# Two matmul groups of a fused FFT and two-layer MoE kernel, issued one and one instead of one after the other

## Chip, cores and metric

One core of a Trainium2 chip runs the whole kernel. The metric is the device time of one execution in microseconds (us); the time before is the median of three runs. Every row below comes from one profiled execution of the kernel before.

## What is computed

The reference takes x of 8 x 3072 x 256 and does three things in turn:

```python
X = np.fft.fft(np.fft.fft(x, axis=1), axis=2).real   # 24576 rows of 256
h = X @ w_in                                         # first layer, 256 -> 2048
x2 = (h - np.tanh(h)) @ w_out                        # 2048 -> 256
h2 = x2 @ w_in2                                      # second layer, 256 -> 1024
solu = h2 * softmax(h2)                              # then a layer norm with gain g_ln
out = layernorm(solu) * g_ln @ w_out2                # 1024 -> 256
```

The weights of the two layers are given as double-precision words and are narrowed in the kernel.

## The kernel before

A first stage of some 195 us does the transform along the sequence and prepares the weights; it is not touched. Then a main loop of 768 steps does both layers (`for step in range(steps + 2)`, L943). The rows of X come in 48 groups of 512 (`n`), and a group takes 16 steps, one for each 128 of the 2048 columns of the first layer (`j` or `m`). A product of two numbers in single precision is made of three passes of the fast 32-bit type: high by high, high by low and low by high (`PASSES`). So every 128-deep product is three matmuls, and each matmul has its own load of weights.

In a step TensorE is given these groups of matmuls, in this order:

- `ab` (L720), 6 matmuls 256 columns wide: the first layer's first product, for this step;
- from `layer2` (L919), by the step's number modulo 4 (`q`): in q = 0 and 1 `h2` (L806), 6 matmuls 512 wide, the second layer's first product for a tile of 128 rows; in q = 2 and 3 `outp` (L896), 12 matmuls 256 wide, the second layer's second product (the output) of an earlier tile, one half of its depth in each of the two steps;
- `o1` (L773), 6 matmuls 512 wide: the first layer's second product, for the step two back. It adds all 16 steps of a group up in two PSUM banks (`x2p`).

The program order is written out by hand (the tile framework is told to keep it), and each engine works its own list in order. What the groups wait for: `o1` reads `gh`, of which ScalarE rounds the high part (L762, shown under its helper's line L152) and GpSimd (POOL) subtracts the low part (L762 through `rest`, L155). The passes of `o1` are high weight, low weight, and last the one with the low part of `gh`, two matmuls each. `outp` reads `ut`, made in the same way in q = 0 and 1 (`split_moved`, L867). At the end of a tile (q = 3) ScalarE scales the output (`o`, L905) and SyncE sends it off (L907). After the last step of a group `o1` copies `x2p` out (L789 to L793: two copies `x2f` and two roundings `x2s` on ScalarE, two subtractions on POOL); this falls in j = 1. In j = 9 and 11 POOL and ScalarE also prepare the input of the next group (`split_z`, L225).

The helper `weave` (L180) takes generators and runs one item of each in turn until all are done. A tail after the loop (L998 to L1024) does the last tiles.

Of the kernel before, what the change touches and what calls it, by code (L numbers as in the profile page):

```python
# [29 lines left out]
NG = B * GPB  # L30
NM = FF1 // P
# [96 lines left out]
def fft2_moe_moe_kernel(  # L128
# [22 lines left out]
    def rnd(o, i):  # L151
        nc.scalar.activation(out=o, in_=i, func=AF.Copy)  # L152

    def rest(eng, o, i, hi):
        eng.tensor_tensor(out=o, in0=i, in1=hi.bitcast(F32), op=ALU.subtract)  # L155
# [24 lines left out]
    def weave(*works):  # L180

        works = list(works)
        while works:
            works = [w for w in works if next(w, works) is not works]
# [366 lines left out]
    def split_wo1(c, raw):  # L551
        rnd(wo1[c][:, 0], raw)
        rest(nc.gpsimd, wo1[c][:, 1], raw, wo1[c][:, 0])
# [74 lines left out]
    def taken(banks, shape, tag, name):  # L628
        banks.append(banks.pop(0))
        return banks[-1].tile(shape, F32, tag=tag, name=name)  # L630
# [134 lines left out]
    def o1(n, m):  # L765
        if m == 0:
            x2p[n] = [p_x2.tile([P, 2 * GP], F32, tag=f"x2_{mt}", name=f"x2p{n}_{mt}") for mt in range(2)]
        gh = gs.pop((n, m))
        c, k = divmod(m, 4)

        for i, (hw, hg) in enumerate(((0, 0), (1, 0), (0, 1))):
            for mt in range(2):
                nc.tensor.matmul(  # L773
                    x2p[n][mt],
                    wo1[c][:, hw, k, mt * P : (mt + 1) * P],
                    gh[:, hg],
                    start=(m == 0 and i == 0),
                    stop=(m == NM - 1 and i == 2),
                )
        if m == NM - 1:  # L780
            xs = wk.tile([P, 2, 2, 2 * GP], F32R, tag="x2s", name=f"x2s{n}")
            x2s[n] = xs
            if n == NG - 1:
                for mt, p in enumerate(x2p.pop(n)):
                    rnd(xs[:, 0, mt], p)
                    rest(nc.vector, xs[:, 1, mt], p, xs[:, 0, mt])
                return
            xf = wk.tile([P, 2, 2 * GP], F32, tag="stage", name=f"x2f{n}")
            for mt, p in enumerate(x2p.pop(n)):  # L789
                rnd(xf[:, mt], p)  # L790
            for mt in range(2):
                rnd(xs[:, 0, mt], xf[:, mt])
                rest(nc.gpsimd, xs[:, 1, mt], xf[:, mt], xs[:, 0, mt])  # L793
# [28 lines left out]
    def soft(n, i):  # L822
        ph, e, st = h2s.pop((n, i)), es.pop((n, i)), sts[n, i]
        u = wk.tile([P, FF2], F32, tag="u", name=f"u{n}_{i}")
        nc.vector.scalar_tensor_tensor(  # L825
            out=u, in0=ph, scalar=1.0, in1=e, op0=ALU.mult, op1=ALU.mult, accum_out=st[:, 2:3]
        )
        nc.vector.tensor_scalar_mul(st[:, 3:4], st[:, 2:3], -1.0 / FF2)
        nc.vector.tensor_scalar_add(st[:, 4:5], st[:, 1:2], 1e-9)
        nc.vector.reciprocal(out=st[:, 5:6], in_=st[:, 4:5])  # L830
        us[n, i] = (u, e)

    def square(n, i):
        u, e = us[n, i]
        st = sts[n, i]
        nc.scalar.activation(out=e, in_=u, func=AF.Square, bias=st[:, 3:4], accum_out=st[:, 6:7])  # L836
        scale(n, i)
# [15 lines left out]
    def turn(n, i):  # L853
        u = us[n, i][0]
        t = mv.tile([P, FF2], F32, tag="t", name=f"tb{n}_{i}")
        nc.vector.transpose(out=t, in_=u)  # L856
        d = mv_d[(4 * n + i) % len(mv_d)]
        nc.sync.dma_start(out=d, in_=t)
        m = mv.tile([P, FF2], F32, tag="m", name=f"um{n}_{i}")
        blocks = d.rearrange("(q p) (k a j) -> a p k q j", q=4, a=4, j=32)  # L860
        for a in range(4):
            nc.sync.dma_start(
                out=m[32 * a : 32 * a + 32].rearrange("p (k q j) -> p k q j", q=4, j=32), in_=blocks[a]
            )
        moved[n, i] = m
# [21 lines left out]
    def outp(n, i, half):  # L887
        if half == 0:
            pos[n, i] = taken(bank_o, [P, 512], "t", f"po{n}_{i}")
        po = pos[n, i]  # L890
        ut = uts.pop((n, i, half))
        for k4 in range(4):
            k = half * 4 + k4
            ks = slice(k4 * P, (k4 + 1) * P)
            for q, (hu, hw) in enumerate(PASSES):
                nc.tensor.matmul(  # L896
                    po[:, :D],
                    ut[:, hu, ks],
                    wo2[:, hw, k],
                    start=(k == 0 and q == 0),  # L900
                    stop=(k == NK2 - 1 and q == 2),
                )
        if half == 1:
            o = wk.tile([P, D], F32, tag="o", name=f"o{n}_{i}")
            nc.scalar.activation(out=o, in_=po[:, :D], func=AF.Copy, scale=sts.pop((n, i))[:, 10:11])  # L905
            r0 = (n * 4 + i) * P
            nc.sync.dma_start(out=out[r0 : r0 + P, :], in_=o)  # L907
            us.pop((n, i))
            pos.pop((n, i))

    def tile_at(step, back):
        t = (step - NM - back) // 4
        return divmod(t, 4) if 0 <= t < 4 * NG else None
# [5 lines left out]
    def layer2(step):  # L919
        q = step % 4  # L920
        at = tile_at(step, 8)
        if at and q == 0:
            square(*at)
            if 4 * at[0] + at[1] <= last_moved:
                turn(*at)
        at = tile_at(step, 12)
        if at:
            if q < 2:
                split_moved(*at, q)
            else:  # L930
                outp(*at, q - 2)
        at = tile_at(step, 4)
        if at:
            if q < 2:
                h2(*at, q)
            elif q == 2:
                expo(*at)
            else:
                soft(*at)

    steps = NG * NM
    out_done = o1_done = 0
    for step in range(steps + 2):  # L943
        n, j = divmod(step, NM)
        if step < steps:
            pab = ab(n, j)
            asb = lead(n, j, pab) if n == 0 else None

        lag = 2 if step < NM else 1
        for s in range(out_done, min(step - lag + 1, steps)):  # L950
            act_out(*divmod(s, NM))
        out_done = max(out_done, min(step - lag + 1, steps))
        if step < steps:
            act_in(n, j, pab, asb or lead(n, j, pab))
        layer2(step)
        s1 = step - 4 if step < NM else step - 2
        for s in (range(o1_done, min(s1 + 1, steps))):
            o1(*divmod(s, NM))
        o1_done = max(o1_done, min(s1 + 1, steps))
        if step in (4, 8):  # L960
            c = (4, 8).index(step) + 2
            split_wo1(c, wo1_raw[c])
        if step == NM:
            raw1.close()
            mv = pool(ctx, "mv", 2, side="right")
        if step in (10, 12):
            split_wi2((step - 10) // 2)
        if step in (2, 3):
            load_wo2(step - 2)
        if step == 6:  # L970
            split_special()
        if 8 <= step < NM:
            gain_wo2(step - 8)
        if NM + 2 < step <= NM + 6:
            special_out(step - NM - 3, pa)
        if step == NM:
            cm = mean_wo2()
        if step == NM + 1:
            for half in range(2):
                center_wo2(half, cm)  # L980
        if NM + 2 <= step < NM + 6:
            pa = special(step - NM - 2)
        if NM + 2 <= step < NM + 4:
            split_wo2(step - NM - 2)
        if j == 6 and 1 <= n and n + 1 < NG:
            load_z(n + 1)
        if 1 <= n and n + 1 < NG and j in (9, 11):
            split_z(n + 1, int(j > 9))
# [9 lines left out]
    tiles = [(NG - 2, 3)] + [(NG - 1, i) for i in range(4)]  # L998
    expo(*tiles[0])
    for f in range(2):  # L1000
        outp(NG - 2, 1, f)
    evict = [trans(NG - 2, 2, f) for f in range(2)]
    for e in evict:
        e()
    for f in range(2):
        outp(NG - 2, 2, f)
    for f in range(2):
        h2(*tiles[1], f)
    soft(*tiles[0])
# [1 line left out]
    for i, at in enumerate(tiles):  # L1011
        evict = [trans(*at, f) for f in range(2)]
        square(*at)
        for e in evict:
            e()
        if i + 2 < len(tiles):
            for f in range(2):
                h2(*tiles[i + 2], f)
        if i + 1 < len(tiles):
            soft(*tiles[i + 1])  # L1020
        if i + 2 < len(tiles):
            expo(*tiles[i + 2])
        for f in range(2):
            outp(*at, f)  # L1024


def thrice(a):
# [45 lines left out]
```

## Time and profile before

| what | value |
|---|---|
| median of 3 runs | 2931.36 us (2930.78 to 2932.79) |
| the profiled execution's own time | 2932.95 us |
| its span in the trace | 2931.2 us |
| TensorE matmuls busy | 98% of the span |
| TensorE weight loads busy | 85% |
| VectorE, ScalarE, POOL busy | 82%, 62%, 67% |

In the rows PE is TensorE's matmuls and PEld its weight loads; DVE is VectorE and ACT ScalarE. A row of the timeline holds instructions of one kind that follow each other: start, length up to the end of the last, and how many. Matmuls are pipelined, so a group's length overlaps the next group's start; what a group takes of the path is the distance from its start to the next group's start.

### The profile page before, as it was taken

The page shows a single profiled execution, that of the slowest core. Times are in us where ns is not written, and L with a number is a line of the kernel's source. Part 1 is how long each engine was busy: PE and PEld are TensorE (multiplying, and loading weights), DVE is VectorE, ACT ScalarE, POOL GpSimd, SP SyncE. Part 2 cuts the span into 40 slices and gives each one's busy share as a digit, 9 for nine tenths or more (in the row PEclk, how much of TensorE's full clock was granted, in tenths as well). Part 3 has the DMA queues.
Part 4 walks back from the last instruction along what each step waited for, and adds up shares of the span by engine and source line. Part 5 has one row for each costly group of instructions (what it writes and reads, how often), then busy time and mean ns, then how long its engine had stood idle before and what let it go on. Part 6 is the DMA issues. An engine that isn't in the chain of part 4 may idle for free. (4 is left out here: it accounts for less than half of the span.)

```text
span 2931.2 us, 49792 instructions
## 1 busy us (share of the span) xinstructions
PE 2882.8 (98%) x16799; PEld 2482.5 (85%) x16799; DVE 2402.9 (82%) x4818; ACT 1804.3 (62%) x3287; POOL 1966.0 (67%) x2413
## 2 busy tenths in 40 slices
PE   7899999999999999999999999999999999999999
PEld 4467888888888888888888888888888888888888
DVE  7897888888888888888888888888888888888885
ACT  2345666666666666666666666666666666666665
POOL 0156767776677776777777767777677766777763
PEclk9999999999999999999999999999999999999999
DMA  8771333443334334344334433433433443443331
GB/s 309 261 285 31 89 92 94 93 94 89 94 87 99 87 89 99 89 93 93 88 94 91 95 89 93 95 90 89 94 93 90 92 92 89 94 97 90 89 91 42
DMA packets 876512, 303.75 MB, mean 104 GB/s; under 512 B 788520, under 2 KB 837688, under 8 KB 872960
## 3 DMA queue, kind: packets, MB, share of 16 engines
q1 hardware_dynamic: 873536, 293.95, 40.7%
q10 hardware_dynamic: 2304, 6.29, 0.5%
q8 instruction: 132, 2.16, 0.3%
q14 instruction: 124, 1.02, 0.1%
q0 software_dynamic: 416, 0.33, 0.0%
HBM read 162.01 MB, written 138.47 MB: 103 GB/s over the span
## 5 line engine op out<-in xcount | busy, mean ns | idle before, releaser
L155 POOL TENSOR_TENSOR gh<-g,gh 128x512 fp32r<-128x512 f32 x768 | 994.3, 1298 | 478.5 <-ACT gh L152 478.5
L773 PE MATMUL x2p<-gh,wo 128*128 128x512 f32 x4608 | 1203.9, 396 | 2.3 <-POOL gh L155 1.7
L773 PEld LDWEIGHTS x2p<-gh,wo 128*128 128x128 f32 x4608 | 838.3, 188 | 180.9 <-POOL gh L155 8.2
L749 ACT ACTIVATE t<-h 128x512 f32<-128x512 f32 x768 | 459.7, 599 | 558.0 <-DVE h L743 456.5
L720 PEld LDWEIGHTS ab<-zs,wt 128*128 128x128 f32 x4608 | 650.1, 188 | 72.8 <-DVE h L743 2.7
L720 PE MATMUL ab<-zs,wt 128*128 128x256 f32 x4608 | 669.1, 280 | 2.1 <-DVE h L743 2.1
L754 DVE TENSOR_TENSOR g<-h,t 128x512 f32<-128x512 f32 x768 | 521.6, 679 | 171.7 <-ACT t L749 168.1
L152 ACT ACTIVATE gh<-g 128x512 fp32r<-128x512 f32 x768 | 481.0, 626 | 235.7 <-DVE g L754 230.7
L806 PE MATMUL ph<-wi,x2s 128*128 128x512 f32 x2304 | 602.8, 397 | 9.7 <-DVE u L825 9.7
L896 PE MATMUL po<-wo,ut 128*128 128x256 f32 x4608 | 592.0, 278 | 3.5 <-ACT ut L152 2.8
L896 PEld LDWEIGHTS po<-wo,ut 128*128 128x128 f32 x4608 | 558.7, 188 | 5.3 <-ACT ut L152 3.5
L727 DVE SCALAR_TENSOR_TENSOR asb<-nb,wnu,ab 128x256 f32<-128x256 f32 x768 | 366.8, 478 | 230.7 <-PE ab L720 230.2
L155 POOL TENSOR_TENSOR ut<-um,ut 128x512 fp32r<-128x512 f32 x372 | 481.7, 1295 | 0.9 <-issue 0.9
L806 PEld LDWEIGHTS ph<-wi,x2s 128*128 128x128 f32 x2304 | 407.7, 189 | 83.6 <-PE ab L720 9.7
L743 DVE TENSOR_TENSOR h<-asb,ab 128x256 f32<-128x256 f32 x768 | 329.3, 429 | 26.5
L742 DVE TENSOR_TENSOR h<-asb,ab 128x256 f32<-128x256 f32 x768 | 329.2, 429 | 26.1
L819 ACT ACTIVATE e<-ph,st 128x1024 f32<-128x1024 f32 x192 | 214.3, 1116 | 98.2 <-DVE st L817 82.6
L817 DVE TENSOR_REDUCE st<-ph 128x1 f32<-128x1024 f32 x192 | 233.5, 1216 | 3.5 <-PE ph L806 3.5
L825 DVE SCALAR_TENSOR_TENSOR u<-ph,e 128x1024 f32<-128x1024 f32 x192 | 233.4, 1216 | 0.0
L152 ACT ACTIVATE ut<-um 128x512 fp32r<-128x512 f32 x372 | 231.0, 621 | 0.0
L856 DVE STREAM_TRANSPOSE tb<-u 128x1024 f32<-128x1024 f32 x186 | 230.1, 1237 | 0.0
L836 ACT ACTIVATE e<-u,st 128x1024 f32<-128x1024 f32 x192 | 219.5, 1143 | 0.0
(101 smaller groups left out, 1529.4 us busy)
## 6 DMA issues: line engine op xcount, KB each, us to landing
mv_d<-tb SPq DMA_DIRECT2D x186, 512.0 KB, 2.6
um<-mv_d SPq DMA_DIRECT2D x744, 128.0 KB, 3.8
out<-o SPq DMA_DIRECT2D x192, 128.0 KB, 1.7
x<-xr SPq DMA_DIRECT2D x23, 1024.0 KB, 8.0
z_d<-zt SPq DMA_DIRECT2D x16, 384.0 KB, 7.2
z_d<-zt ACTq DMA_DIRECT2D x16, 384.0 KB, 7.1
wo<-w_out SPq DMA_DIRECT2D x24, 256.0 KB, 5.3
zf<-z_d SPq DMA_DIRECT2D x48, 128.0 KB, 3.4
```

The lines of the kernel that those rows point to most:

```text
L152: nc.scalar.activation(out=o, in_=i, func=AF.Copy)
L155: eng.tensor_tensor(out=o, in0=i, in1=hi.bitcast(F32), op=ALU.subtract)
L720: nc.tensor.matmul(pab[:, u], wt[c][:, hw, u, o : o + P], zs[:, hz, u], start=(i == 0), stop=(i == 2))
L727: nc.vector.scalar_tensor_tensor(out=asb, in0=zg[n][1], scalar=wnu[:, m : m + 1], in1=pab[:, 0], op0=ALU.mult, op1=ALU.add)
L742: nc.vector.tensor_tensor(out=h[:, 0], in0=asb, in1=pab[:, 1], op=ALU.add)
L743: nc.vector.tensor_tensor(out=h[:, 1], in0=asb, in1=pab[:, 1], op=ALU.subtract)
L749: nc.scalar.activation(out=t, in_=h, func=AF.Tanh)
L754: nc.vector.tensor_tensor(out=g, in0=hs.pop((n, m)).rearrange("p u n -> p (u n)"), in1=ts_.pop((n, m)).rearrange("p u n -> p (u n)"), op=A ...
L773: nc.tensor.matmul(x2p[n][mt], wo1[c][:, hw, k, mt * P : (mt + 1) * P], gh[:, hg], start=(m == 0 and i == 0), stop=(m == NM - 1 and i == 2),)
L806: nc.tensor.matmul(ph[:, fs], xs[:, hx, k, tk], wi2[:, hw, k, fs], start=(k == 0 and q == 0), stop=(k == 1 and q == 2),)
L817: nc.vector.tensor_reduce(out=st[:, 0:1], in_=ph, axis=AX.X, op=ALU.max, negate=True)
L896: nc.tensor.matmul(po[:, :D], ut[:, hu, ks], wo2[:, hw, k], start=(k == 0 and q == 0), stop=(k == NK2 - 1 and q == 2),)
```

## The change

`outp` and `o1` become generators that yield after each matmul. In a step with `outp` (q = 2 and 3), `layer2` issues the first four of its 12 matmuls and hands the rest back; the loop then issues the rest in turn with `o1`. The order on TensorE goes from 12 `po` matmuls and then 6 `x2p` matmuls to this: 5 `po`; then x2p, po five times over; then the sixth x2p; then the last two po. Whatever follows a generator's last matmul (the output's scaling and store, the copying out of `x2p`) is issued when that generator ends. Everywhere else `run` issues the generator in one go, as before.

```diff
@@ o1 @@
                     stop=(m == NM - 1 and i == 2),
                 )
+                yield
@@ outp @@
                     stop=(k == NK2 - 1 and q == 2),
                 )
+                yield
...
+    def run(work):
+        for _ in work:
+            pass
@@ layer2 @@
         at = tile_at(step, 12)
+        work = None
         if at:
             if q < 2:
                 split_moved(*at, q)
             else:
-                outp(*at, q - 2)
+                work = outp(*at, q - 2)
+                for _ in range(4):
+                    next(work)
...
+        return work
@@ main loop @@
-        layer2(step)
+        work = layer2(step)
         s1 = step - 4 if step < NM else step - 2
         for s in (range(o1_done, min(s1 + 1, steps))):
-            o1(*divmod(s, NM))
+            sums1 = o1(*divmod(s, NM))
+            if work is None:
+                run(sums1)
+            else:
+                weave(work, sums1)
+                work = None
+        if work is not None:
+            run(work)
@@ tail, three times @@
-        outp(NG - 2, 1, f)
+        run(outp(NG - 2, 1, f))
```

## Rows read from the trace of the kernel before

**Rows 1.** The page's busy times: us, share of the span, instructions.
```profile
PE 2882.8 (98%) x16799; PEld 2482.5 (85%) x16799; DVE 2402.9 (82%) x4818; ACT 1804.3 (62%) x3287; POOL 1966.0 (67%) x2413
```

**Rows 2.** Timeline of PE over steps j = 7, 8 and 10: start us, length us, matmuls.
```profile
1499.83 0.87 PE L720 MATMUL ab<-zs,wt 128*128 128x256 f32 x6
1500.54 1.54 PE L896 MATMUL po<-wo,ut 128*128 128x256 f32 x12
1501.92 1.56 PE L773 MATMUL x2p<-gh,wo 128*128 128x512 f32 x6
1503.32 0.87 PE L720 MATMUL ab<-zs,wt 128*128 128x256 f32 x6
1504.03 1.56 PE L806 MATMUL ph<-wi,x2s 128*128 128x512 f32 x6
...
1510.34 0.87 PE L720 MATMUL ab<-zs,wt 128*128 128x256 f32 x6
1511.04 1.54 PE L896 MATMUL po<-wo,ut 128*128 128x256 f32 x12
1512.41 1.56 PE L773 MATMUL x2p<-gh,wo 128*128 128x512 f32 x6
1513.82 0.87 PE L720 MATMUL ab<-zs,wt 128*128 128x256 f32 x6
```

**Rows 3.** Waits from 300 to 2800 us: total us, times, longest us.
```profile
PE ph L806 <- DVE u L825: 6.1, 21, 0.6
PEld x2p L773 <- POOL gh L155: 4.1, 16, 0.5
```

**Rows 4.** Timeline of PE and PEld around 1512.7 us, inside an x2p group.
```profile
1512.41 0.63 PE L773 MATMUL x2p<-gh,wo 128*128 128x512 f32 x2
...
1512.65 0.19 PEld L773 LDWEIGHTS x2p<-gh,wo 128*128 128x128 f32 x1
```

**Rows 5.** Timeline of PE near 259 us: matmuls only 8 columns wide.
```profile
258.63 1.40 PE L697 MATMUL pa<-zh,wt 128*128 128x8 f32 x12
259.88 0.95 PE L720 MATMUL ab<-zs,wt 128*128 128x256 f32 x6
```

**Rows 6.** Timeline of PE in the tail: a run of 24 po matmuls.
```profile
2908.26 2.99 PE L896 MATMUL po<-wo,ut 128*128 128x256 f32 x24
2911.09 1.04 PE L881 MATMUL pt<-ident,u 128*128 128x128 f32 x8
```

**Rows 7.** Timeline of PE, plain f32 products: 16 from 234.03, the last 4 from 236.62.
```profile
234.03 3.61 PE L666 MATMUL cm<-wg,ones 128*128 128x256 f32 x16
...
236.62 1.03 PE L666 MATMUL cm<-wg,ones 128*128 128x256 f32 x4
```

**Rows 8.** Timeline of one step j = 3 near 1432 us (group 22).
```profile
1431.41 2.56 POOL L155 TENSOR_TENSOR gh<-g,gh 128x512 fp32r<-128x512 f32 x2
...
1431.88 1.62 PE L773 MATMUL x2p<-gh,wo 128*128 128x512 f32 x6
...
1432.77 0.30 PEld L773 LDWEIGHTS x2p<-gh,wo 128*128 128x128 f32 x2 [0.24 <-POOL gh L155]
...
1433.34 0.87 PE L720 MATMUL ab<-zs,wt 128*128 128x256 f32 x6
```

**Rows 9.** Timeline of another step j = 3 near 1544 us (group 24).
```profile
1541.24 2.57 POOL L155 TENSOR_TENSOR x2s<-x2f,x2s 128x512 fp32r<-128x512 f32 x2
1543.76 1.29 POOL L155 TENSOR_TENSOR gh<-g,gh 128x512 fp32r<-128x512 f32 x1
...
1544.88 0.43 PEld L773 LDWEIGHTS x2p<-gh,wo 128*128 128x128 f32 x2
```

**Rows 10.** Timeline of ACT around the end of step j = 7.
```profile
1502.74 0.47 ACT L905 ACTIVATE o<-po,st 128x256 f32<-128x256 f32 x1
1504.37 0.63 ACT L152 ACTIVATE gh<-g 128x512 fp32r<-128x512 f32 x1 [1.17 <-DVE g L754]
```

**Rows 11.** Timeline of ACT and PE at a group's start, j = 1 to 2.
```profile
1482.27 1.08 ACT L152 ACTIVATE x2f<-x2p 128x512 f32<-128x512 f32 x2
...
1484.38 1.56 PE L773 MATMUL x2p<-gh,wo 128*128 128x512 f32 x6
```

More of the change, by code (lines that the diff above doesn't have):

```diff
@@ L1005, in fft2_moe_moe_kernel @@
     for f in range(2):
-        outp(NG - 2, 2, f)
+        run(outp(NG - 2, 2, f))
     for f in range(2):
@@ L1023, in fft2_moe_moe_kernel @@
         for f in range(2):
-            outp(*at, f)
+            run(outp(*at, f))
 def thrice(a):
```

## The prediction

> **What bounds the kernel now.** I read the page's busy times first. TensorE's matmuls fill 98% of the span and no other engine is above 82% [rows 1]. So the question is whether TensorE itself gets through the same matmuls faster, and whether the new order makes it wait. The timeline of TensorE comes next [rows 2]. The reader is to see that its groups follow each other without a gap. From start to start, `ab` takes 0.71, 0.71 and 0.70 us, so 0.118 us for one matmul 256 columns wide. `po` takes 1.38 and 1.37 us for 12 of the same width, 0.1146 each. `x2p` takes 1.40 and 1.41 us, 0.234 for one of 512 columns. Whatever shortens a step must lower one of these three prices. The list of waits says what else there is [rows 3]: in 2500 us `h2` waits 21 times for VectorE's `u`, and 16 times the load of an `x2p` matmul waits for POOL's `gh`. `po` itself never stands there.
>
> **What moves.** No instruction is added or dropped. The change acts in steps with `outp`: the loop reaches it from step 30 to step 767, in two steps of every four, so 370 steps; the tail keeps its order. In each, `po` 0 to 4 stay ahead, six `x2p` are each followed by a `po`, and `po` 11 closes the step. The Python does what the text says: one matmul per item, and `o1` is resumed past its sixth, so nothing is lost.
>
> **Step 1, the price of the matmuls.** A gain would need the loads to run differently. The load of the third `x2p` matmul starts at 1512.65, while the second started at 1512.64 (0.63 us for two less some 0.40 for one, from 1512.41) [rows 4]. It is not earlier, although the load before it was long done: matmuls that are only 8 columns wide come 1.25 / 12 = 0.104 us apart, and that is then what a load takes [rows 5]. So one set of weights is held ahead and no more. A 256-wide matmul at 0.115 to 0.118 is just over its 0.104 load; a 512-wide one at 0.234 covers its load twice. Alternating gives the 512-wide matmul's spare 0.13 us to nobody, because the load after next can't start in it.
>
> What alternation itself costs no row shows directly. The nearest are the two prices of the 256-wide matmul: 0.1146 in runs of 12 between other groups, 0.118 in `ab`, which is a run of only 6 next to 512-wide ones. A run of 24 in the tail also shows 2.83 / 24 = 0.118 [rows 6], so the lower price isn't sure even in a long run. I take 0.118 for all 12 `po`, since a run of one is nearest to the short run, and leave `x2p` at 0.234: 12 x (0.1178 - 0.1146) = 0.038 us a step, x 370 = **+14 us**. The bounds: at best every matmul at the cheapest row (`po` 1.37 / 12 = 0.114, `x2p` 1.40 / 6 = 0.233) gains about 0.015 us a step, -6 us; at worst `po` at 0.120 and `x2p` at 0.238 (half a hundredth of a us over the rows, which is their spread) loses 0.09 a step, +32 us.
>
> Here the trace has to be weighed against a rule. The rows show a load that starts with the matmul before its own and never sooner [rows 4]. The Trainium skill, page "TensorE: Matmul & The Clock Gate", section "Step-by-step: what each phase is for", says that TensorE's 64-deep window pulls weight loads ahead of matmuls in flight when they target the background buffer; read freely, that would let loads pile up under the 512-wide matmuls. With that page's spacing of columns / 2.4 + 2.5 ns a pair would cost 0.325 us where I count 0.352.
>
> **Step 2, POOL's `gh`.** The low half of `gh` is used by the fifth and sixth `x2p` matmul, and the wait stands on the fifth one's load. In step j = 3 POOL has only just made it, behind two subtractions for `x2s` and another `gh` [rows 8, 9]. Before, that load starts with the fourth `x2p`: 0.71 + 1.375 + 3 x 0.234 = 2.79 us into the step. After, it starts with `po` 8: 0.71 + 5 x 0.118 + 4 x 0.234 + 3 x 0.118 = 2.59. It is 0.20 earlier, or 0.16 when the longer step j = 2 just before is allowed for. It also has less room: before, the matmul in front lasts 0.234, so a load of 0.104 may be 0.13 late at no cost; after, the matmul in front is a `po` and 0.014 is left.
>
> In group 22 POOL ends its first `gh` at about 1432.7 (half of 2.56 us after 1431.41) and the load follows at 1432.77, some 0.06 later; by its own order it would have started at 1431.88 + 0.70 = 1432.58, so it is 0.19 late, of which 0.06 shows (the group takes 1.46 instead of 1.40) [rows 8]. That is the 0.13 again. In the new order it is 0.35 late and 0.34 shows: 0.28 more. In group 24 POOL ends at 1545.05 and the load starts in its order, at 1545.12 (0.43 us for two less 0.19 for one, from 1544.88), so it has 0.01 to spare over those 0.06 [rows 9]; in the new order it is 0.15 late and 0.14 shows. Sixteen waits of the first kind are on record [rows 3], and the other 30 or so groups are like the second: 16 x 0.28 + 30 x 0.14 = **+8.7 us**. Nothing if POOL turns out to be ahead by 0.16 us, and twice as much if it is as late in every group as in group 22 and the alternation is cheap.
>
> **Step 3, what costs nothing.** `o1` in j = 2 starts after 5 `po` instead of 12, 0.8 us sooner, and must find `x2p` copied out: the copies end at 1483.35 and the first `x2p` started at 1484.38 [rows 11], so 0.2 us are left, about 0.1 for the load in front of it. If that cover went, it would be some 0.1 us in 47 groups, 5 us. The output's scaling on ScalarE waits for the last `po`, which now comes at the end of the step, some 1.4 us later; behind it ScalarE's next work is a `gh` that starts 1.05 us into the next step, after a wait of 1.17 for VectorE [rows 10, 2]. The scaling of 0.47 us fits into that wait, and the store behind it on SyncE's queue moves with it; nobody waits for either. `po`'s bank is next taken three steps later.
>
> **Step 4, a small return.** The 21 waits of `h2` for `u` [rows 3] come in j = 12, after two steps that are now 0.04 us longer each. If VectorE doesn't slip with them, 21 x 0.08 come back: I take **-1.5 us**, between -1.7 and 0.
>
> **Sum.** 14 + 8.7 - 1.5 = +21 us. On the profiled execution's 2932.95 us that is 2954; that execution was 1.6 us above the median, so 2952.5 on the median's scale, which I give as **2953**.
>
> **Rivals.** About 0.2% (6 us) is what a measurement of this kernel can tell from no change.
>
> - *The order is neutral for TensorE.* Prices stay at 0.1146 and 0.234 and only POOL's `gh` bites, from a step 0.20 us earlier, not 0.16: 46 x 0.04 = 1.8 us more than above, 8.7 + 1.8 = +10.5, so 2942. For it: the groups' prices vary by 0.01 us with no visible reason. Against it: the short runs of 256-wide matmuls are all at 0.118.
> - *Loads run ahead, and it is faster.* If the load after next could start under a 512-wide matmul, only columns would count. Plain f32 products of 256 columns come (236.62 - 234.03) / 12 = 0.216 us apart [rows 7]; taken as two passes, that is an estimate of 0.216 for 512 columns in one pass and 0.108 for 256. A pair then costs 0.324 instead of 0.349, 6 x 0.025 x 370 = -55 us, and the sooner fifth `x2p` adds some 5 to the 10 of POOL: 2891. It decides from the point where PEld rows start more than 0.01 us ahead of the matmul before theirs. Against it stands [rows 4].
> - *The cheapest rows everywhere.* -6 from step 1 and +10 from POOL: 2936, no change that can be told.
> - *Alternation is dear.* 0.120 and 0.238: +32 and +8, 2971. For it: such prices stand at the upper edge of what single groups show.
>
> **How the numbers follow.** Forecast 0.47, neutral order 0.19, dear alternation 0.11, cheapest rows 0.12, loads ahead 0.11. Slower by over 0.2% takes the first three, less a little for a neutral order with a milder POOL: 0.75. The same: 0.13. Faster: 0.12. The range leaves out the loads ahead and the dear end: 2934 to 2966.
>
> **What would show it.** Right: in TensorE's timeline a step j = 6 or 7 goes from 3.48 and 3.49 us to about 3.52; in j = 3 the `x2p` loads wait for POOL in nearly every group, 0.14 to 0.35 us each, some 10 us in the list of waits where 4.1 stands now; `o` on ScalarE sits in the first 0.8 us of the next step with no one behind it. Wrong: a pair of `x2p` and `po` under 0.345 us from start to start, or PEld rows ahead of the matmul before theirs.

## The result and the profile after

The changed kernel takes 2949.68 us (median of 4 runs, 2948.44 to 2951.74), beside 2932.07 us for the kernel before (median of 4). The ratio is 1.0056, with a 95% interval from 1.0043 to 1.0068: slower by 17.6 us, where +21 us was forecast. Its profiled execution took 2951.74 us, with a span of 2950.0 us; the span of before was 2931.2.

The page's busy times, which answer to [rows 1], show the same picture: TensorE is still the busiest engine, with 98% of the span.

```profile
PE 2900.2 (98%) x16799; PEld 2492.6 (84%) x16799; DVE 2408.8 (82%) x4818; ACT 1822.3 (62%) x3287; POOL 1964.4 (67%) x2413
```

The timeline of TensorE over the steps j = 6 and 7 of a group answers to [rows 2]:

```profile
1505.73 0.87 PE L720 MATMUL ab<-zs,wt 128*128 128x256 f32 x6
1506.43 0.74 PE L897 MATMUL po<-wo,ut 128*128 128x256 f32 x5
1507.01 0.40 PE L773 MATMUL x2p<-gh,wo 128*128 128x512 f32 x1
1507.24 0.28 PE L897 MATMUL po<-wo,ut 128*128 128x256 f32 x1
1507.36 0.40 PE L773 MATMUL x2p<-gh,wo 128*128 128x512 f32 x1
...
1508.77 0.40 PE L773 MATMUL x2p<-gh,wo 128*128 128x512 f32 x1
1509.00 0.40 PE L897 MATMUL po<-wo,ut 128*128 128x256 f32 x2
1509.24 0.87 PE L720 MATMUL ab<-zs,wt 128*128 128x256 f32 x6
...
1512.76 0.86 PE L720 MATMUL ab<-zs,wt 128*128 128x256 f32 x6
```

A pair is one `x2p` and the `po` behind it. Five pairs lie between the first `x2p` and the sixth: 1508.77 - 1507.01 = 1.76 us, 0.352 a pair, just what the forecast counted. The two steps take 3.51 and 3.52 us; in [rows 2] a step with `outp` takes 3.48 and 3.49.

The list of waits from 300 to 2800 us (total us, times, longest us) answers to [rows 3]:

```profile
ACT o L907 <- PE po L897: 116.0, 155, 1.2
...
PEld x2p L773 <- POOL gh L155: 12.1, 44, 0.5
...
PE ph L807 <- DVE u L826: 4.6, 21, 0.2
...
PE x2p L773 <- POOL gh L155: 0.3, 2, 0.2
```

The `x2p` load now waits for POOL in nearly every group (44 times instead of 16), `h2` waits a little less for `u`, and ScalarE's output scaling waits for the last `po`, as it should.

Where the time went can be read step by step. The table gives the mean length of a step, from its first `ab` matmul to that of the next step in the trace, over groups 4 to 46, in ns. The last columns belong to the experiments below.

```
steps                     before   after  skip_j3  only_j3   lead8  four_two
j = 2, 6, 10, 14 (mean)   3477.9  3510.9   3511.9   3477.7  3498.0    3506.6
j = 7, 11, 15 (mean)      3493.3  3520.0   3520.0   3493.3  3513.4    3500.0
j = 3                     3519.1  3745.0   3498.7   3795.7  3520.0    3490.0
j = 12                    3762.5  3721.7   3720.8   3756.5  3729.0    3741.0
the other seven (mean)    3507.8  3504.6   3505.8   3506.6  3507.8    3508.4
a whole group            56227.5 56602.9  56367.8  56488.6 56335.3   56316.7
```

After minus before is 375 ns a group, 17.3 us over 46 groups. The price is 4 x 33 + 3 x 26.7 in the woven steps outside j = 3, and another 27 that may be put down to j = 3 (taken over from its neighbours, not measured there): 239 ns, 11.0 us. The rest of j = 3, 226 - 27 = 199 ns or 9.2 us, is the wait for POOL. The step j = 12 gives 41 ns back (-1.9 us) and the other seven 22 (-1.0 us).

One late step in detail: j = 3 of group 23, TensorE and POOL together (as [rows 8] of before).

```profile
1496.46 2.53 POOL L155 TENSOR_TENSOR gh<-g,gh 128x512 fp32r<-128x512 f32 x2
...
1497.21 0.40 PE L773 MATMUL x2p<-gh,wo 128*128 128x512 f32 x1
...
1497.45 0.28 PE L897 MATMUL po<-wo,ut 128*128 128x256 f32 x1
1497.79 0.19 PEld L773 LDWEIGHTS x2p<-gh,wo 128*128 128x128 f32 x1 [0.39 <-POOL gh L155]
1497.80 0.50 PE L773 MATMUL x2p<-gh,wo 128*128 128x512 f32 x1
...
1498.25 0.39 PE L773 MATMUL x2p<-gh,wo 128*128 128x512 f32 x1
```

The load of the fifth `x2p` would have begun with the `po` at 1497.45. It begins at 1497.79, some 0.05 us after the end of POOL's first `gh` (about half of 2.53 us from 1496.46; 1497.74 in the trace). From the fourth `x2p` (1497.21) to the sixth (1498.25) it is 1.04 us instead of two pairs, 0.70: the whole 0.34 us shows, since the matmul in front of the load is a short one.

### The profile page after: what moved, and what is told of

It reads as the page before. It is cut to its first block, busy times and chain, and to the rows that moved or that the text cites. A ratio compares the mean times of both kernels' runs of the same rounds, so it can differ in the third digit from the quotient of the medians.

```text
span 2950.0 us, 49793 instructions
## 1 busy us (share of the span) xinstructions
PE 2900.2 (98%) x16799; PEld 2492.6 (84%) x16799; DVE 2408.8 (82%) x4818; ACT 1822.3 (62%) x3287; POOL 1964.4 (67%) x2413
## 5 line engine op out<-in xcount | busy, mean ns | idle before, releaser
L773 PE MATMUL x2p<-gh,wo 128*128 128x512 f32 x4608 | 1426.4, 397 | 3.8 <-POOL gh L155 2.1
L773 PEld LDWEIGHTS x2p<-gh,wo 128*128 128x128 f32 x4608 | 863.3, 188 | 208.3 <-POOL gh L155 17.2
L897 PE MATMUL po<-wo,ut 128*128 128x256 f32 x4608 | 964.5, 280 | 3.5 <-ACT ut L152 2.8
L897 PEld LDWEIGHTS po<-wo,ut 128*128 128x128 f32 x4608 | 752.9, 188 | 20.8 <-ACT ut L152 3.5
L720 PEld LDWEIGHTS ab<-zs,wt 128*128 128x128 f32 x4608 | 625.2, 189 | 38.1 <-DVE h L743 2.7
```

Of the source, the lines that this page charges most:

```text
L720: nc.tensor.matmul(pab[:, u], wt[c][:, hw, u, o : o + P], zs[:, hz, u], start=(i == 0), stop=(i == 2))
L773: nc.tensor.matmul(x2p[n][mt], wo1[c][:, hw, k, mt * P : (mt + 1) * P], gh[:, hg], start=(m == 0 and i == 0), stop=(m == NM - 1 and i == 2),)
L897: nc.tensor.matmul(po[:, :D], ut[:, hu, ks], wo2[:, hw, k], start=(k == 0 and q == 0), stop=(k == NK2 - 1 and q == 2),)
```

## The experiments

Each ran on one chip beside the kernel before, whose median was 2933.89 us in the first four, 2932.29 in the next four and 2934.17 in the last three.

**Without j = 3 (skip_j3).** The changed kernel, but where POOL is late the old order stays:

```diff
             sums1 = o1(*divmod(s, NM))
+            if work is not None and j == 3:
+                run(work)
+                work = None
             if work is None:
```

> The changed kernel, but in steps j = 3 (one of 16, where POOL's gh is late) the output matmuls go ahead of o1 as before. Theory: two costs that add up, a dearer price of the alternating matmuls (0.027 to 0.034 us in each of the eight woven steps of a group, of which some 0.02 comes back in the steps between and 0.04 in j = 12) and POOL's wait in j = 3 (0.19 us more a group). Without j = 3, 7 x 0.03 - 0.065 = 0.148 us a group are left, x 46 = +7 us over the kernel before, ratio 1.0024, and the list shows the waits of x2p's loads for POOL as before (about 4 us). Rival: POOL's backlog is the bound and its wait only moves to another step: +14 us or more, ratio 1.005.

Measured: 2941.15 us, ratio 1.0021 (1.0012 to 1.0030), +7 us. The list of waits:

```profile
PEld x2p L773 <- POOL gh L155: 3.3, 16, 0.5
```

Sixteen waits, as before, and the other woven steps keep their 3512 and 3520 ns. So the wait for POOL isn't moved to another step; it is a cost by itself, and what is left is the price of the matmuls.

**Only j = 3 (only_j3).** The reverse, with `j != 3` in the same place.

> The reverse: woven in steps j = 3 alone, 47 steps of 370. Theory: the wait for POOL comes in full, 0.19 us a group and 0.03 more since the step before is no longer longer, and the price of one woven step, 0.027: 0.25 x 46 = +11.5 us, ratio 1.004. Rival (the loss is a matter of alternation as such, everywhere alike): 47/370 of 17.6, +2 us, ratio 1.001.

Measured: 2945.06 us, ratio 1.0041 (1.0028 to 1.0053), +11 us from 46 steps of 370 (the first woven step is j = 14 of group 1, so j = 3 is woven in groups 2 to 47; the 47 of the expectation is one too many).

```profile
PEld x2p L773 <- POOL gh L155: 14.4, 45, 0.5
```

The loss isn't spread over the alternation. The two partial changes together cost 7 + 11 us and the whole costs 17.6. In the table j = 3 grows by 277 ns here and by 226 in the full change: the woven step j = 2 in front of it, longer by 34 in the full change, gives POOL that much more time. Some 17 of the 51 ns are left without an account.

**Eight ahead instead of four (lead8).**

```diff
-                for _ in range(4):
+                for _ in range(8):
                     next(work)
```

> Eight output matmuls are issued ahead instead of four: 9 po, then x2p and po in turn three times, then three x2p. Theory: the fifth x2p's load starts with the fourth x2p again, 2.8 us into the step as before, so the wait for POOL goes back to 4 us; only the last four po of a step are dear, 4 x 0.004 x 370 = +6 us, less 1 that comes back in j = 12: ratio 1.0015. Rival (any alternation upsets TensorE for the whole step): 0.030 us a step as with four ahead, +10 us, ratio 1.0034. Rival (the loads profit and only POOL spoiled it): faster than before, ratio 0.998.

Measured: 2938.78 us, ratio 1.0016 (1.0008 to 1.0025), which is the first theory's figure. Its reason fits only in part: by the mean distances of a step j = 7 (groups 4 to 46), `po` takes 8 ns more than before and `x2p` 13 ns more, where the theory had 16 ns in `po` alone. The list of waits:

```profile
PEld x2p L773 <- POOL gh L155: 0.5, 2, 0.3
```

The waits fell to 0.5 us and not to 4. POOL's `gh` ends mostly 0.02 to 0.06 us sooner in the step than before, and the load's own place is 0.02 later. In group 22 the load starts 0.12 us after the fourth `x2p` where it was 0.20 before, and the 0.234 us of that matmul hide all of it: the step takes 3.51 us, as its neighbours without lateness do. Even with almost nothing of POOL's wait left, putting matmuls of the two kinds in turn won nothing; that loads profit and only POOL spoiled it is ruled out.

**Four and two (four_two).** The lead of four stays, and in the loop:

```diff
-                weave(work, sums1)
+                if j == 3:
+                    run(work)
+                else:
+                    for _ in range(2):
+                        for w in (sums1, sums1, work, work, work, work):
+                            next(w)
+                run(sums1)
+                run(work)
```

> Four po, two x2p, three times over (steps j = 3 as before). Half as many changes between the widths as in the woven order. Theory (a po is cheap only from about the fifth in a row on, so that all 12 are at 0.118): the same +7 us as without j = 3, ratio 1.0024. Rival (the price is one of the change from one width to the other): half of it, +3 us, ratio 1.001.

Measured: 2937.49 us, ratio 1.0013 (1.0004 to 1.0022), which is the rival's figure; the theory's 1.0024 lies outside the interval, but the 1.0021 that skip_j3 measured lies inside. The timeline of a step j = 7 says more:

```profile
1562.03 0.62 PE L897 MATMUL po<-wo,ut 128*128 128x256 f32 x4
1562.49 0.63 PE L773 MATMUL x2p<-gh,wo 128*128 128x512 f32 x2
1562.95 0.64 PE L897 MATMUL po<-wo,ut 128*128 128x256 f32 x4
1563.42 0.63 PE L773 MATMUL x2p<-gh,wo 128*128 128x512 f32 x2
1563.89 0.63 PE L897 MATMUL po<-wo,ut 128*128 128x256 f32 x4
1564.36 0.63 PE L773 MATMUL x2p<-gh,wo 128*128 128x512 f32 x2
```

The four `po` at the start take 0.46 us, 0.115 each; the two runs of four behind an `x2p` take 0.47, 0.1175 each. So once the run is broken the low price doesn't return within four. In the table j = 2, 6, 10, 14 are as dear as in the full change (+29 against +33), but j = 7, 11, 15 only +7: there the low price was already reached in `ab` and carried into `po`. Neither theory is right as it was put.

**Equal widths (narrow_before, narrow_after).** In both kernels, `o1` is cut to 256 columns in 15 of a group's 16 steps, which leaves half of the first layer's second product out. Each was executed once, and only distances between matmuls are read:

```diff
+        wd = 2 * GP if m == 0 else GP
...
-                    x2p[n][mt],
+                    x2p[n][mt][:, :wd],
...
-                    gh[:, hg],
+                    gh[:, hg, :wd],
```

> The kernel before, with o1 cut to half its columns in 15 of a group's 16 steps, so that x2p is 256 columns wide as po is (half of the first layer's second product is left out). Base for the next run: po in a row at 0.113 after the first few, x2p at 0.113 to 0.118 each; TensorE may wait for VectorE, so the distances between matmuls are read, not the time.

> The changed kernel with the same cut (half of the first layer's second product is left out), so po and x2p alternate at equal width. If the price of alternating is one of the change of width, po and x2p in turn come 0.113 to 0.114 apart, as po in a row. If it comes from changing weights' tile and PSUM bank at each matmul, they come 0.117 to 0.120 apart.

The timeline of a step j = 7, first of the old order, then of the alternation:

```profile
1472.24 0.86 PE L720 MATMUL ab<-zs,wt 128*128 128x256 f32 x6
1472.94 1.53 PE L897 MATMUL po<-wo,ut 128*128 128x256 f32 x12
1474.30 0.87 PE L774 MATMUL x2p<-gh,wo 128*128 128x256 f32 x6
1475.01 0.28 PE L720 MATMUL ab<-zs,wt 128*128 128x256 f32 x1
```

```profile
1476.62 0.87 PE L720 MATMUL ab<-zs,wt 128*128 128x256 f32 x6
1477.32 0.74 PE L898 MATMUL po<-wo,ut 128*128 128x256 f32 x5
1477.91 0.28 PE L774 MATMUL x2p<-gh,wo 128*128 128x256 f32 x1
...
1479.19 0.40 PE L898 MATMUL po<-wo,ut 128*128 128x256 f32 x2
1479.43 0.28 PE L720 MATMUL ab<-zs,wt 128*128 128x256 f32 x1
```

In the old order 12 `po` take 1.36 us, 0.113 each, and `x2p`, of the same width now and with nothing in between, 0.71 / 6 = 0.118. In turn, the 11 matmuls from 1477.91 to 1479.19 come 0.116 apart, which is between the two bands that were expected, nearer the upper one. The step grows from 2.77 to 2.81 us. Steps j = 6 and 7 have no change of width here and the loss of 0.04 us is there, so the width isn't its cause. Only a third of it lies in the alternation itself: by mean distances over groups 4 to 46, the last seven `po` and the six `x2p` take 16 ns more together, `ab` 8 more, and the first five `po` 21 more, though they stand in a row in both kernels. In the old order they find the low price already reached in `ab`; here they don't.

**The PSUM bank (narrow_bank_runs, bank_pairs).** Is it the change of bank? `x2p` goes to two PSUM banks in turn, so the bank changes with each matmul. The first run is narrow_before with three `x2p` to one bank and then three to the other. The second is the kernel before at full width, with three changes of bank in six matmuls instead of five; its edit:

```diff
-        for i, (hw, hg) in enumerate(((0, 0), (1, 0), (0, 1))):
-            for mt in range(2):
+        halves = ((0, 0), (1, 0), (0, 1))
+        for mt, i in ((0, 0), (0, 1), (1, 0), (1, 1), (0, 2), (1, 2)):
+            for hw, hg in (halves[i],):
```

> The kernel before with the same cut of o1 to half its columns in 15 of 16 steps, and o1's six matmuls ordered so that three in a row go to one PSUM bank and then three to the other, instead of bank by bank in turn. If the price comes from changing the bank at each matmul, x2p comes 0.113 to 0.114 apart but for one; if it comes from the weights' tile, still 0.117 to 0.118. Only the distances between matmuls are read.

> The kernel before, full width, with o1's passes ordered so that the bank changes three times in six matmuls instead of five; the two passes with the low half of gh stay last, so POOL has as long as before. If a change of bank costs 4 ns, two fewer in 768 steps give 6 us back: ratio 0.998. If not: 1.000.

In the first, a step j = 7 takes 2.77 us again, and the distances of its six `x2p` starts in the trace are 117, 120, 119, 117, 115 and 118 ns, the same as with a change at each matmul. The second took 2933.74 us, ratio 0.9996 (0.9987 to 1.0005). The bank isn't it either. What the expectation leaves over, the weights' tile, doesn't set the price alone: the 24 `po` of the tail [rows 6] read tiles of the same names as those at 0.113 and come 0.118 apart. No run here varies the tile.

**POOL relieved (x2s_dve).** The changed kernel, with the second `x2s` subtraction on VectorE:

```diff
-                rest(nc.gpsimd, xs[:, 1, mt], xf[:, mt], xs[:, 0, mt])
+                rest(nc.vector if mt else nc.gpsimd, xs[:, 1, mt], xf[:, mt], xs[:, 0, mt])
```

> The changed kernel, but the second of the two x2s subtractions of a group goes to VectorE, so POOL gets to the gh of step j = 3 1.28 us sooner. Theory: POOL's lateness is all there is to the wait in j = 3, so it goes in every group and the price of the eight woven steps stays: 17.6 less 9 is +8.5 us over the kernel before, ratio 1.003. Rival: VectorE, with 0.68 us more in j = 2, is late for the next step and TensorE's ab or h2 waits for it instead: no better than 1.005.

Measured: 3028.78 us, ratio 1.0325 (1.0311 to 1.0339), far beyond what either had expected. Both were right in part. The step j = 3 takes 3520 ns, as the other woven steps do, and no wait of an `x2p` load for POOL is on the list: POOL's backlog was all there was to that wait. But VectorE pays. Two rows of its timeline and TensorE's, from one group:

```profile
1592.12 0.85 DVE L155 TENSOR_TENSOR x2s<-x2f,x2s 128x512 fp32r<-128x512 f32 x1 [3.32 <-ACT x2s L152]
```

```profile
1599.21 1.18 PE L807 MATMUL ph<-wi,x2s 128*128 128x512 f32 x4 [1.31 <-DVE u L826]
```

The added instruction costs 0.85 us, but it stands at the head of VectorE's list for 3.32 us until ScalarE has rounded, and everything behind it is late; in j = 4 the step is 1.76 us longer than before (5263 ns against 3503).

**The wait in j = 12 (before_z1011).** The forecast's step 4 took the wait of `h2` for `u` as given. In the kernel before, ScalarE stands 3.35 us at the rounding `zs` of the next group's input and waits for POOL's `zc`, the exponential `e` comes behind it, and in j = 12 `h2` waits for VectorE's `u`, which reads `e`:

```profile
1513.64 0.42 ACT L152 ACTIVATE zs<-zc 128x256 fp32r<-128x256 f32 x1 [3.35 <-POOL zc L233]
...
1514.96 1.11 ACT L819 ACTIVATE e<-ph,st 128x1024 f32<-128x1024 f32 x1
...
1518.45 1.64 PE L806 MATMUL ph<-wi,x2s 128*128 128x512 f32 x6 [0.27 <-DVE u L825]
```

Here that rounding is put behind the exponential, in the kernel before:

```diff
-        if 1 <= n and n + 1 < NG and j in (9, 11):
-            split_z(n + 1, int(j > 9))
+        if 1 <= n and n + 1 < NG and j in (10, 11):
+            split_z(n + 1, int(j > 10))
```

> The kernel before, with the first half of the next group's preparation (split_z) moved from the end of step j = 9 to the end of j = 10, behind the exponential on ScalarE's list. Theory: the wait in j = 12 (0.26 us a group, some 12 us in all, and the -2 us that the change got back there) comes from ScalarE standing at that preparation for POOL; out of the exponential's way it goes: ratio 0.996, faster than both kernels. Rival: ScalarE then stands in j = 11 and VectorE's u is as late: ratio 1.000.

Measured: 2921.93 us, ratio 0.9962 (0.9949 to 0.9974): faster than both kernels. ScalarE's timeline around j = 10:

```profile
1506.70 1.11 ACT L819 ACTIVATE e<-ph,st 128x1024 f32<-128x1024 f32 x1 [0.55 <-DVE st L817]
...
1507.81 0.41 ACT L152 ACTIVATE zs<-zc 128x256 fp32r<-128x256 f32 x1
1508.12 0.62 ACT L152 ACTIVATE gh<-g 128x512 fp32r<-128x512 f32 x1
```

The rounding `zs` now follows `e` and finds its input ready. In the list of waits `h2` no longer stands, and j = 12 takes 3502.5 ns like its neighbours, 260 less than before.

**Both together (z1011_pairs).**

> Both: split_z's first half at the end of j = 10 and the new order of o1's passes. 0.996 by the former alone, 0.994 if the bank's price is real.

Measured: 2923.00 us, ratio 0.9959 (0.9946 to 0.9973). The new order of `o1`'s passes adds nothing.

## Why the prediction was right

**Step 1, the price.** The main argument held: the loads don't run further ahead. TensorE's weight loads in a woven step, from the timeline of the changed kernel:

```profile
1507.01 0.19 PEld L897 LDWEIGHTS po<-wo,ut 128*128 128x128 f32 x1
1507.25 0.19 PEld L773 LDWEIGHTS x2p<-gh,wo 128*128 128x128 f32 x1
1507.37 0.19 PEld L897 LDWEIGHTS po<-wo,ut 128*128 128x128 f32 x1
```

Each stands within 0.01 us of the start of the matmul before its own (1507.01, 1507.24 and 1507.36 above). From 300 to 2800 us of this trace none of some 14,800 loads starts before that matmul does. The 512-wide matmuls' spare time stays unused, and the pair costs 0.352 us.

An estimate by the spacing that the Trainium skill gives, page "TensorE: Matmul & The Clock Gate", section "Back-to-back issue gap" (columns / 2.4 + 2.5 ns), is 0.325 us a pair. The trace doesn't agree. Of the 0.027 us that it shows beyond the estimate, 0.018 lie in the 512-wide matmul (0.234 against 0.216), whose load is covered, so a limit on the loads isn't the reason for most of it.

The size of a load was misread. Of the 12 matmuls in [rows 5] the first two start 28 ns apart, and all later ones 111 or 112 in the trace, so a load takes some 0.112 us and not 0.104. A 256-wide matmul at 0.113 only just covers it. The covers that step 2 counts with shrink by 0.008 us each, from 0.13 to 0.12 and from 0.014 to 0.006, which changes little there.

That the new price is about the 0.118 of `ab` came out, at 0.027 to 0.034 us a step instead of 0.038: 11.0 us instead of 14. It comes together in another way than was forecast, so that the sum is this near is in part luck. By mean distances in j = 10, the first four `po` cost what they did. The other eight rise from 0.114 to 0.117, where all 12 were counted from 0.1146 to 0.1178. The six `x2p`, which were left at their price, take 5 ns more together. The reason that was given, short runs, is only partly right: four_two and the narrow kernels show that a low price has to be reached and can be carried over from the group before, and neither the width nor the bank is what breaks it. What sets it stays open.

**Step 2, POOL.** 8.7 us were forecast and 9.2 measured. The two kinds of group are there: the median j = 3 of the groups that waited before goes from 3556 to 3854 ns, that of the others from 3493 to 3665, so 0.271 and 0.145 us without the price of 0.027 (0.28 and 0.14 forecast). The examples agree: 0.34 us in group 23, and for the other kind, in group 25 for one, the distance from the fourth `x2p` to the sixth is 849 ns in the trace, 0.145 more than two pairs (0.14 forecast). skip_j3, only_j3 and x2s_dve each show by themselves that this term stands apart from the first.

**Step 3, the free parts.** They were free. `o` on ScalarE now runs at the start of the next step and the `gh` behind it still has 0.34 us of its wait for VectorE left:

```profile
1512.96 0.48 ACT L907 ACTIVATE o<-po,st 128x256 f32<-128x256 f32 x1 [0.71 <-PE po L897]
1513.78 0.64 ACT L152 ACTIVATE gh<-g 128x512 fp32r<-128x512 f32 x1 [0.34 <-DVE g L754]
```

In j = 2, where `x2p` must have been copied out 0.8 us sooner, the step takes what j = 10 takes (3512 ns both).

**Step 4, the return.** -1.9 us, a little more than the -1.7 that was given as its end, and partly by chance. In the trace 21 groups are late in j = 12, as the list said, with a median of 4.02 us before and 3.97 after: each gives back some 0.055 us and not 0.08. One group that took 4.33 us before gives 0.37 by itself. Another -1.0 us in the seven steps without `outp` wasn't foreseen.

**The rivals.** The neutral order falls, since skip_j3 is 7 us slower with no more waits for POOL than before. The dear alternation falls too (0.352 a pair and not 0.358), and with it the cheapest rows everywhere (0.114 + 0.233 = 0.347). Loads that run ahead aren't in the rows above, and would have shown in lead8, which has almost no wait for POOL left and is slower than before.

## What to carry to other kernels

When TensorE is busy throughout, its time is the sum of the distances between matmuls. Before putting wide and narrow matmuls in turn to hide weight loads, look in the trace at when a load starts: here it starts with the matmul before its own, so a wide matmul covers one load and no more. Reordering the bound engine also moves the moment at which it needs its inputs: work out for each wait how much earlier its load comes and how long the matmul in front of it is, because a short one hides far less lateness. And an instruction moved to an engine with time to spare can cost far more than its length if it stands at the head of that engine's list waiting.

## What was not expected of the hardware

The distance between 256-wide matmuls has two main levels, about 0.113 and 0.118 us. In the kernel before, each place of the step j = 7 repeats within 2 ns from group 4 to 46. In narrow_before, `po` runs at 0.113 and `x2p` of the same width at 0.118, whatever the order of its banks. In bank_pairs the six full-width distances in j = 7 (229, 234, 235, 233, 232 and 237 or 238 ns) are the same in either order of passes, so they go with the place in the stream and not with the pass. Which property of the stream sets the level wasn't found, and no run here isolates it.
